# w_out, g and w_in in one buffer, with layer 2's places 64 bytes further on, in a retention and two-layer kernel

## The chip, the cores and the metric

One core of a Trainium2 chip (trn2) runs the whole program. The metric is device time in microseconds (us) from start to end of one execution; lower is better.

## The reference

Retention attention (4 batches, 8 heads, 576 positions, head size 64) gives x, 2304 tokens by 512; two feed-forward layers follow. All is float32 for the caller.

```python
scores = scale * np.matmul(q, k.transpose(0, 1, 3, 2))
x = np.matmul(scores * Dmat, v)        # Dmat: gamma ** (row - column), 0 above the diagonal
h = x @ w_in;  g = np.maximum(0.01 * h, h);  x = g @ w_out       # layer 1, d_ff = 2048
h = x @ w_in2; g = h - np.tanh(h);           out = g @ w_out2    # layer 2
```

The weights come as float64 words and are narrowed to float32 on the chip.

## The kernel before

Every float32 product of the layers is made of three matmuls on float32r parts: a high part times a high part, high times low, low times high. So each tile of w_in, w_out and g holds two parts of 512 columns (1,024 floats, 4 KB a partition). x lies in `xh` and `xl`, 4 planes of 2,304 tokens, for the whole program; `acc` holds the sums of a layer over groups.

The d_ff axis is cut into 16 slices of 128, in 4 groups of 4 (`GF`). A step is one (layer m, group g, token block, slice f). Token blocks are 512 wide, and one is 256 wide (tokens 2048 to 2303). `h_mm` (L255, matmul at L262) makes h of a step with 12 matmuls: weights are w_in, the streamed operand is x. `act_a` (L330) and `chain` (L362) make g on ScalarE, VectorE and GpSimd. `o_mm` (L381, matmul at L404) multiplies with w_out: in layer 1 the weights are w_out and g is streamed (512 or 256 columns); in layer 2 the weights are parts of g and w_out is streamed (512 columns). `evac` (L439) adds the result to acc, after the last slice of a group.

In layer 2 the 512-wide blocks from token 512 on are *folded* (`h_folded`, L268): two steps' h are made together from sums of x's and w_in's parts, with 256-column matmuls at L296, in runs of 6, 12 or 18, and the pending `o_mm` is issued in halves between them (L958 to L987). The folded sums of x are formed from acc by `fold_x` (L411, L427 to L430).

The order on TensorE is the loop at L938: for each step h_mm, then the pending o_mm `lag` steps back (2 in layer 1, 3 in layer 2, `due` at L925), then evac and the planned pieces of weight work. During retention (L517) the first 6 x 256 tokens of group 0 of layer 1 are already done in units (`unit_h`, L721; `unit_o`, L746) between the pairs of heads.

Places in SBUF: `wi` (L80) holds 8 tiles of w_in and 64 spare floats; `w_place` (L82) gives layer 2's tiles, and those of layer 1's group 0, a lead of `LEAD` = 16 floats (64 bytes), the others none. w_out has a ring of 4 tiles (`wring`), g one of 3 (`g1`), and retention's g one of 2 (`g0`), each from its own pool. All these tiles have sizes that are multiples of 128 bytes.

Raw float64 pieces come by DMA on the SP queue (`load_piece`, L127). Those of layer 1's group 0 land in a part of acc that isn't used yet (from token 1280 on); all others in staging pools: `stage` (2 tiles) while retention runs, `stage1` (3 tiles) in the layers. `narrow_ops` (L138) narrows a piece: ScalarE at L152, VectorE at L158, L163 and twice at L169. `split_into` (L241) makes the two parts on ScalarE (L242) and GpSimd (L243). Eight pieces of layer 2's w_out (`early_kept`, L247) are narrowed and split during retention and written to DRAM (`keep_out`, L188), to be fetched again in layer 2 (`fetch`, L218).

Of the kernel before, what the change touches and what calls it, by code (L numbers as in the profile page):

```python
# [35 lines left out]
def retention_moe_moe(  # L36
# [27 lines left out]
    NG = NF // GF  # L64

    keep = ctx.enter_context(tc.tile_pool(name="keep", bufs=1))
    wring = ctx.enter_context(tc.tile_pool(name="wring", bufs=GF))
    ctx.enter_context(tc.tile_pool(name="edge", bufs=1, side="right")).tile(
        [P, 80], F32, name="edge"
    )  # L70
    pools = {}
    narrow = ctx.enter_context(ExitStack())
    pools["st"] = narrow.enter_context(tc.tile_pool(name="stage", bufs=2, side="right"))

    qb = keep.tile([P, 4], F32, name="qb")
    xh = keep.tile([P, KK, NT], F32R, name="xh")
    xl = keep.tile([P, KK, NT], F32R, name="xl")
    acc = keep.tile([P, KK * NT], F32, name="acc")
    acc_t = acc.rearrange("p (d t) -> p d t", d=KK)
    wi = keep.tile([P, 8 * 1024 + 64], F32R, name="wi")  # L80

    def w_place(m, g, j):  # L82
        at = (4 + j) * 1024 if m == 0 else j * 1024
        at += LEAD if m or g == 0 else 0
        return wi[:, at:at + 1024].rearrange("p (i c) -> p i c", i=2)

    HALF = 256
    xe, early_tiles = {}, {}
# [27 lines left out]
    def lag(s):  # L116
        return 2 if steps[s][0] == 0 else 3
# [9 lines left out]
    def load_piece(key):  # L127
        m, kind, f = key
        src = ((w1i, w1o), (w2i, w2o))[m][kind][f]
        if m or key[2] >= GF:  # L130
            st = pools["st"].tile([P, 512], I64 if wide else F32, tag="st", name="st")
        else:
            spare = acc_t[:, len(raw_at) % 4, NT - (1024 if wide else 512):]
            raw_at[key] = st = spare.bitcast(I64 if wide else F32)
        nc.sync.dma_start(out=st, in_=src)
        raw[key] = st

    def narrow_ops(key):  # L138

        if not wide:  # L140
            def only():
                w = cw_pool[0].tile([P, 512], F32, tag="cw", name="cw")
                nc.vector.tensor_copy(out=w, in_=raw.pop(key))
                half[key] = w
            return [only]
        t = {}

        def begin():
            words = raw.pop(key).bitcast(U32).rearrange("p (n t) -> p n t", t=2)
            t["lo"], t["hi"] = words[:, :, 0], words[:, :, 1]  # L150
            t["w"] = cw_pool[0].tile([P, 512], U32, tag="cw", name="cw")
            nc.scalar.activation(  # L152
                out=t["w"].bitcast(F32), in_=t["hi"].bitcast(F32), func=AF.Abs
            )

        def clamp():
            wf = t["w"].bitcast(F32)
            nc.vector.tensor_scalar(  # L158
                out=wf, in0=wf, scalar1=F64_LO, scalar2=F64_HI, op0=ALU.max, op1=ALU.min
            )  # L160

        def shift():
            nc.vector.tensor_scalar(  # L163
                out=t["w"], in0=t["w"], scalar1=3, scalar2=0x3FFFFFF8,
                op0=ALU.logical_shift_left, op1=ALU.bitwise_and,
            )

        def join(src, scalar, op):
            nc.vector.scalar_tensor_tensor(  # L169
                out=t["w"], in0=t[src], scalar=scalar, in1=t["w"], op0=op, op1=ALU.bitwise_or  # L170
            )

        def top():
            join("hi", 0xC0000000, ALU.bitwise_and)

        def low():
            join("lo", 29, ALU.logical_shift_right)
            half[key] = t["w"].bitcast(F32)

        return [begin, clamp, shift, top, low]  # L180

    def keep_split(key, wf):
        at = len(kept) % 4 * 1024
        sp = wi[:, at:at + 1024].rearrange("p (i c) -> p i c", i=2)
        split_into(sp, wf)
        kept[key] = sp

# [30 lines left out]
    def fetch(key):  # L218
        if len(key) == 2:
            j, f = key  # L220
            wp = w_place(1, 0, f % GF // 2 * 4 + 2 + j)
            ws.setdefault(f, {})[j] = wp
        else:
            m, kind, f = key
            wp = wt[key] = (
                wring.tile([P, 2, 512], F32R, tag="wo", name="wp") if kind
                else w_place(1, 0, f % GF // 2 * 4 + f % 2)
            )
        nc.sync.dma_start(out=wp.bitcast(F32), in_=kept[key])

    def split_piece(key):
        wf = half.pop(key)
        m, kind, f = key
        if kind:
            wp = wring.tile([P, 2, 512], F32R, tag="wo", name="wp")
        else:
            wp = w_place(m, f // GF, f % GF)
        split_into(wp, wf)
        wt[key] = wp
# [28 lines left out]
    def h_folded(s):  # L268
# [58 lines left out]

        return first, first_rest, first_sum, second, second_sum, third, fourth

    def act_a(s, tight=False):  # L330
        m, g, t0, n, f = steps[s]
        W, tp = pools["w"], pools["t"]
        h = hp[s][:, :n]
        if m == 0:
            gt = pools["g"].tile([P, 2, W], F32R, tag="g", name="g")
            nc.scalar.activation(out=gt[:, 0, :n], in_=h, func=AF.Prelu, alpha=0.01)  # L336
            nc.scalar.activation(out=h, in_=h, func=AF.Prelu, alpha=0.01)
            tmp[s] = gt
            return
        u = tp.tile([P, W], F32, tag="u", name="u", bufs=3)  # L340
        v = u if tight else tp.tile([P, W], F32, tag="u", name="v", bufs=3)
        q = pools["t2"].tile([P, W], F32, tag="q", name="q", bufs=1)
        t_, mk = early_tiles.pop(s, None) or [
            pools["t2"].tile([P, W], F32, tag=x, name=x) for x in ("t", "mk")
        ]
        nc.scalar.activation(out=u[:, :n], in_=h, func=AF.Square)  # L346
        nc.scalar.activation(out=t_[:, :n], in_=h, func=AF.Tanh)  # L347

        def cube():
            nc.gpsimd.tensor_tensor(out=v[:, :n], in0=t_[:, :n], in1=u[:, :n], op=ALU.mult)  # L350

        if not tight:
            cube()
        nc.scalar.activation(
            out=q[:, :n], in_=u[:, :n], func=AF.Square, scale=math.sqrt(RHO_C), bias=qb[:, 0:1]
        )
        nc.scalar.activation(out=mk[:, :n], in_=u[:, :n], func=AF.Relu, bias=qb[:, 1:2])
        if tight:
            cube()
        tmp[s] = (v, t_, q, mk)  # L360

    def chain(s):  # L362
        m, g, t0, n, f = steps[s]
        h = hp.pop(s)[:, :n]
        if m == 0:
            v, gt = h, tmp.pop(s)
        else:
            v, t_, q, mk = (x[:, :n] for x in tmp.pop(s))
            nc.vector.tensor_tensor(out=h, in0=h, in1=t_, op=ALU.subtract)  # L369
            nc.vector.scalar_tensor_tensor(  # L370
                out=v, in0=q, scalar=RHO_A, in1=v, op0=ALU.add, op1=ALU.mult
            )
            nc.vector.copy_predicated(out=v, mask=mk.bitcast(U32), data=h)  # L373
            gt = pools["g"].tile([P, 2, pools["w"]], F32R, tag="g", name="g")
            nc.scalar.activation(out=gt[:, 0, :n], in_=v, func=AF.Copy)  # L375
        (nc.gpsimd if m else nc.vector).tensor_tensor(  # L376
            out=gt[:, 1, :n], in0=v, in1=gt[:, 0, :n].bitcast(F32), op=ALU.subtract
        )
        ga[s] = gt

    def o_mm(s, part=None):  # L381
# [12 lines left out]
        for d in {None: range(cnt), 0: range(cnt // 2), 1: range(cnt // 2, cnt)}[part]:  # L394
# [2 lines left out]
            o = ps[d // pack][:, at:at + width]  # L397
            for i, (wi, gi) in enumerate(((0, 0), (0, 1), (1, 0))):
                if m == 0:
                    l, r = w[:, wi, ds], gt[:, gi, :n]  # L400
                else:
                    l, r = gt[:, gi, ds], w[:, wi, :]

                nc.tensor.matmul(  # L404
                    out=o, lhsT=l, rhs=r,
                    start=f == 0 and i == 0 and d % pack == 0,
                    stop=f == GF - 1 and i == 2 and (d + 1) % pack == 0,
                    skip_group_check=pack > 1,
                )
# [107 lines left out]
    def retention():  # L517
        with ExitStack() as ac:
            ak = ac.enter_context(tc.tile_pool(name="ak", bufs=1))
            ap_ = ac.enter_context(tc.tile_pool(name="ap", bufs=3))  # L520
            g0_ = ac.enter_context(tc.tile_pool(name="g0", bufs=2))
            cw_pool[0] = ac.enter_context(tc.tile_pool(name="c0", bufs=2))
            ps_s = ac.enter_context(tc.tile_pool(name="ps_s", bufs=1, space=PSUM))
            ps_a = ac.enter_context(tc.tile_pool(name="ps_a0", bufs=1, space=PSUM))
# [189 lines left out]
            def unit_h(u):  # L714
                t0, f0 = place(u)
                for f in range(2):
                    w = wt[0, 0, f0 + f]
                    for kk in range(KK):
                        cs = slice(kk * P, (kk + 1) * P)
                        for j, (wi, x) in enumerate(((0, xh), (0, xl), (1, xh))):  # L720
# [2 lines left out]
                                start=f == 0 and kk == 0 and j == 0,  # L723
                                stop=f == 1 and kk == KK - 1 and j == 2, skip_group_check=True,
                            )
                gt = g0_.tile([P, 2, 2, QW], F32R, tag="g", name="g")
                nc.scalar.activation(out=gt[:, 0], in_=x_b, func=AF.Prelu, alpha=0.01)
                nc.scalar.activation(out=x_b, in_=x_b, func=AF.Prelu, alpha=0.01)
                nc.vector.tensor_tensor(
# [117 lines left out]
    def layers():  # L847
        with ExitStack() as mc:
            pools["t"] = mc.enter_context(tc.tile_pool(name="t1", bufs=2))
            pools["g"] = mc.enter_context(tc.tile_pool(name="g1", bufs=3))  # L850
            pools["st"] = narrow.enter_context(tc.tile_pool(name="stage1", bufs=3, side="right"))
            cw_pool[0] = narrow.enter_context(
                tc.tile_pool(name="c1", bufs=2 * GF + 4, side="right")
# [69 lines left out]
            done = [n_early]  # L923

            def due(s):  # L925
                return n_early <= done[0] <= s - lag(s) and done[0] < end - GF

            def extras(s, quick):
                ops = plan.get(s, [])
# [134 lines left out]
```

## Time and profile before

| | |
|---|---|
| time, median of 3 runs | 876.88 us (876.71 to 878.21) |
| time of the profiled execution | 876.76 us |
| its span, first to last instruction | 875.0 us |
| TensorE (PE) busy | 857.5 us, 98% |
| VectorE, ScalarE, GpSimd busy | 587.6, 445.6, 365.0 us |
| DMA, mean over the span | 125 GB/s |

The profile is one execution. PE is TensorE's matmul, PEld its weight load, which runs beside it; a matmul's recorded duration overlaps the next one's, so PE's pace is read from how far apart matmuls start. The granted clock is 9 tenths or more of 2.4 GHz in all 40 slices of the page, 0.999 in the mean.

### The profile page before, as it was taken

What the parts mean: (1) busy time and instruction counts of PE and PEld (TensorE: products, weight loads), DVE (VectorE), ACT (ScalarE), POOL (GpSimd) and SP (SyncE); (2) the same over time, 40 slices, a digit from 0 to 9 for tenths busy, and PEclk for the clock granted to TensorE, in tenths of its full rate; (3) what the DMA queues carried; (4) which work ended last, traced back from release to release, by engine and by line L of the source; (5) the groups of instructions that cost most, each with busy time, mean ns of one, the idle gap of its engine ahead of it and who ended that gap; (6) DMA issues with size and microseconds to landing.
All of it is one profiled execution on the core that took longest, in us unless ns stands there. A gap on an engine that the chain in (4) does not pass through costs nothing.

```text
span 875.0 us, 14820 instructions
## 1 busy us (share of the span) xinstructions
PE 857.5 (98%) x5584; PEld 744.8 (85%) x5584; DVE 587.6 (67%) x1006; ACT 445.6 (51%) x888; POOL 365.0 (42%) x297
## 2 busy tenths in 40 slices
PE   6999999999999999999999999999999999999997
PEld 5889999888988888888888888888898889889886
DVE  5996776687685777658745567754666566656665
ACT  4553454453345334454534566665666556665663
POOL 2642222140046203273334756554455545453553
PEclk9999999999999999999999999999999999999999
DMA  9835663333455433654534200260004300261112
GB/s 336 316 120 181 207 206 133 133 120 121 145 193 209 153 120 108 230 193 114 208 111 145 97 1 1 73 211 7 1 25 146 119 1 1 73 217 49 49 49 73
DMA packets 36471, 109.23 MB, mean 125 GB/s; under 512 B 4144, under 2 KB 5680, under 8 KB 36400
## 3 DMA queue, kind: packets, MB, share of 16 engines
q1 hardware_dynamic: 35968, 108.08, 35.9%
q8 instruction: 44, 0.72, 0.3%
q10 hardware_dynamic: 432, 0.20, 0.1%
q14 instruction: 27, 0.22, 0.1%
HBM read 78.39 MB, written 29.88 MB: 124 GB/s over the span
## 4 chain that ended last, share of the span: by engine, by line
PE 89%; DVE 5%; DMA 2%; issue 1%; POOL 1%; ACT 1%; SPq 0%; POOLq 0%; DVEq 0%; ACTq 0%
PE a L404 40%; PE h L262 26%; PE h L296 12%; PE a L746 3%; PE x_b L721 3%; PE o L671 1%; DMA cm_sb<-in_cmask 1%; PE sc L595 1%; PE o L660 1%; DVE cw L169 1%; DMA acc<-in_w1i 1%; DVE pt L609 1%; PE x_c L628 0%; DVE acc L467 0%; DVE xl L482 0%
## 5 line engine op out<-in xcount | busy, mean ns | idle before, releaser
L262 PE MATMUL h<-xh,wi 128*128 128x512 f32 (+1 forms) x800 | 229.7, 356 | 0.0
L404 PE MATMUL a<-wp,g 128*128 128x512 f32 x864 | 220.4, 393 | 0.9 <-POOL g L376 0.5
L404 PEld LDWEIGHTS a<-wp,g 128*128 128x128 f32 x864 | 154.5, 188 | 29.5 <-POOL g L376 1.2
L243 POOL TENSOR_TENSOR wi<-cw,wi 128x512 fp32r<-128x512 f32 x64 | 89.8, 1420 | 214.0 <-ACT wi L242 188.3
L404 PE MATMUL a<-g,wp 128*128 128x512 f32 (+1 forms) x816 | 175.9, 364 | 0.6 <-DVE g L376 0.6
L404 PEld LDWEIGHTS a<-g,wp 128*128 128x128 f32 x816 | 141.4, 189 | 25.6 <-DVE g L376 0.8
L262 PEld LDWEIGHTS h<-xh,wi 128*128 128x128 f32 x800 | 143.6, 188 | 22.5
L262 PE MATMUL h<-xl,wi 128*128 128x512 f32 (+1 forms) x400 | 142.4, 356 | 0.0
L350 POOL TENSOR_TENSOR v<-t,u 128x512 f32<-128x512 f32 (+1 forms) x76 | 92.4, 1216 | 92.4 <-ACT t L347 90.5
L376 POOL TENSOR_TENSOR g<-v,g 128x512 fp32r<-128x512 f32 (+1 forms) x76 | 95.7, 1259 | 80.8 <-ACT g L375 80.8
L336 ACT ACTIVATE g<-h 128x512 fp32r<-128x512 f32 (+1 forms) x68 | 37.2, 548 | 166.4 <-PE h L262 124.5
L169 DVE SCALAR_TENSOR_TENSOR cw<-st,cw 128x512 uint32<-128x512 uint32 x112 | 99.0, 884 | 2.9
L370 DVE SCALAR_TENSOR_TENSOR v<-q,v 128x512 f32<-128x512 f32 (+1 forms) x76 | 54.7, 720 | 49.9 <-POOL v L350 49.6
L262 PEld LDWEIGHTS h<-xl,wi 128*128 128x128 f32 x400 | 75.5, 189 | 11.4
L467 DVE TENSOR_TENSOR acc<-a,acc 128x512 f32<-128x512 f32 (+1 forms) x114 | 70.9, 658 | 21.0 <-PE a L404 21.0
L375 ACT ACTIVATE g<-v 128x512 fp32r<-128x512 f32 (+1 forms) x76 | 45.4, 597 | 75.5 <-DVE v L373 68.1
L346 ACT ACTIVATE u<-h 128x512 f32<-128x512 f32 (+1 forms) x80 | 44.0, 550 | 78.0 <-DVE h L290 53.9
L296 PE MATMUL h<-xh,wi 128*128 128x256 f32 x384 | 75.6, 281 | 0.5 <-DVE v L373 0.3
L369 DVE TENSOR_TENSOR h<-h,t 128x512 f32<-128x512 f32 (+1 forms) x80 | 51.5, 644 | 33.7 <-ACT t L347 32.9
L158 DVE TENSOR_SCALAR cw<-cw 128x512 f32<-128x512 f32 x64 | 34.1, 533 | 57.8 <-ACT cw L152 57.7
L296 PEld LDWEIGHTS h<-xe,wi 128*128 128x128 f32 x432 | 60.2, 188 | 8.5 <-DVE mk L290 2.4
L296 PEld LDWEIGHTS h<-xh,wi 128*128 128x128 f32 x384 | 61.9, 188 | 2.9 <-DVE v L373 1.8
(86 smaller groups left out, 1244.5 us busy)
## 6 DMA issues: line engine op xcount, KB each, us to landing
kept<-wi SPq DMA_DIRECT2D x48, 512.0 KB, 3.9
wi<-kept SPq DMA_DIRECT2D x32, 512.0 KB, 4.6
st<-in_w2o SPq DMA_DIRECT2D x16, 512.0 KB, 5.9
st<-in_w2i SPq DMA_DIRECT2D x16, 512.0 KB, 3.7
wp<-kept SPq DMA_DIRECT2D x16, 512.0 KB, 3.7
st<-in_w1i SPq DMA_DIRECT2D x12, 512.0 KB, 4.3
st<-in_w1o SPq DMA_DIRECT2D x12, 512.0 KB, 3.4
kv<-in_vn SPq DMA_DIRECT2D x16, 320.0 KB, 5.3
```

Source lines behind the costliest of these rows:

```text
L169: nc.vector.scalar_tensor_tensor(out=t["w"], in0=t[src], scalar=scalar, in1=t["w"], op0=op, op1=ALU.bitwise_or)
L243: nc.gpsimd.tensor_tensor(out=wp[:, 1, :], in0=wf, in1=wp[:, 0, :].bitcast(F32), op=ALU.subtract)
L262: nc.tensor.matmul(out=ps[:, :n], lhsT=w[:, wi, cs], rhs=x[:, kk, t0:t0 + n], start=kk == 0 and i == 0, stop=kk == KK - 1 and i == 2,)
L296: nc.tensor.matmul(out=out_, lhsT=w[:, wi_, at:at + P], rhs=x(xi, kk), start=start and kk == 0 and j == 0, stop=stop and kk == 1 and j == ...
L346: nc.scalar.activation(out=u[:, :n], in_=h, func=AF.Square)
L350: nc.gpsimd.tensor_tensor(out=v[:, :n], in0=t_[:, :n], in1=u[:, :n], op=ALU.mult)
L369: nc.vector.tensor_tensor(out=h, in0=h, in1=t_, op=ALU.subtract)
L370: nc.vector.scalar_tensor_tensor(out=v, in0=q, scalar=RHO_A, in1=v, op0=ALU.add, op1=ALU.mult)
L375: nc.scalar.activation(out=gt[:, 0, :n], in_=v, func=AF.Copy)
L376: (nc.gpsimd if m else nc.vector).tensor_tensor(out=gt[:, 1, :n], in0=v, in1=gt[:, 0, :n].bitcast(F32), op=ALU.subtract)
L404: nc.tensor.matmul(out=o, lhsT=l, rhs=r, start=f == 0 and i == 0 and d % pack == 0, stop=f == GF - 1 and i == 2 and (d + 1) % pack == 0, s ...
L467: nc.vector.tensor_tensor(out=dst, in0=a, in1=dst, op=ALU.add)
```

## The change

`wi`, `wring`, `g0` and `g1` become one tile `w` of 15 slots of 1,024 floats and a lead: 4 for w_out, 3 for g, 8 for w_in. w_out's and g's slots are taken in turn by two counters. In layer 2 both are used with the lead of 16 floats, as w_in already was; in layer 1 without. A g of a 256-wide block of layer 1 is written with the lead inside its slot; retention's g takes two of the g slots, with the lead. The raw pieces of `early_kept` land in acc's last 512 tokens, each over two planes, in two turns, and the pool `stage` goes. `due` takes the lag from the pending step's layer and not from the current one's.

```diff
--- before.py
+++ after.py
@@ -64,25 +64,36 @@
     NG = NF // GF
 
     keep = ctx.enter_context(tc.tile_pool(name="keep", bufs=1))
-    wring = ctx.enter_context(tc.tile_pool(name="wring", bufs=GF))
     ctx.enter_context(tc.tile_pool(name="edge", bufs=1, side="right")).tile(
         [P, 80], F32, name="edge"
     )
     pools = {}
     narrow = ctx.enter_context(ExitStack())
-    pools["st"] = narrow.enter_context(tc.tile_pool(name="stage", bufs=2, side="right"))
 
     qb = keep.tile([P, 4], F32, name="qb")
     xh = keep.tile([P, KK, NT], F32R, name="xh")
     xl = keep.tile([P, KK, NT], F32R, name="xl")
     acc = keep.tile([P, KK * NT], F32, name="acc")
     acc_t = acc.rearrange("p (d t) -> p d t", d=KK)
-    wi = keep.tile([P, 8 * 1024 + 64], F32R, name="wi")
+    N_OUT, N_G, N_IN = GF, 3, 8
+    wide_all = keep.tile([P, (N_OUT + N_G + N_IN) * 1024 + LEAD], F32R, name="w")
+
+    def slot(k, lead):
+        at = k * 1024 + (LEAD if lead else 0)
+        return wide_all[:, at:at + 1024].rearrange("p (i c) -> p i c", i=2)
 
     def w_place(m, g, j):
-        at = (4 + j) * 1024 if m == 0 else j * 1024
-        at += LEAD if m or g == 0 else 0
-        return wi[:, at:at + 1024].rearrange("p (i c) -> p i c", i=2)
+        return slot(N_OUT + N_G + (4 + j if m == 0 else j), m or g == 0)
+
+    turn = {"o": 0, "g": 0}
+
+    def w_out_place(m):
+        turn["o"] += 1
+        return slot((turn["o"] - 1) % N_OUT, m)
+
+    def g_place(m):
+        turn["g"] += 1
+        return slot(N_OUT + (turn["g"] - 1) % N_G, m)
 
     HALF = 256
     xe, early_tiles = {}, {}
@@ -127,11 +138,20 @@
     def load_piece(key):
         m, kind, f = key
         src = ((w1i, w1o), (w2i, w2o))[m][kind][f]
-        if m or key[2] >= GF:
+        if key in early_kept:
+            k = 2 * (len(raw_at) % 2)
+            raw_at[key] = True
+            if wide:
+                st = acc_t[:, k:k + 2, NT - 512:].bitcast(I64)
+                src = src.rearrange("p (a n) -> p a n", a=2)
+            else:
+                st = acc_t[:, k, NT - 512:]
+        elif m or key[2] >= GF:
             st = pools["st"].tile([P, 512], I64 if wide else F32, tag="st", name="st")
         else:
             spare = acc_t[:, len(raw_at) % 4, NT - (1024 if wide else 512):]
-            raw_at[key] = st = spare.bitcast(I64 if wide else F32)
+            raw_at[key] = True
+            st = spare.bitcast(I64 if wide else F32)
         nc.sync.dma_start(out=st, in_=src)
         raw[key] = st
 
@@ -146,11 +166,17 @@
         t = {}
 
         def begin():
-            words = raw.pop(key).bitcast(U32).rearrange("p (n t) -> p n t", t=2)
-            t["lo"], t["hi"] = words[:, :, 0], words[:, :, 1]
-            t["w"] = cw_pool[0].tile([P, 512], U32, tag="cw", name="cw")
+            st = raw.pop(key).bitcast(U32)
+            t["w"] = t["as"] = cw_pool[0].tile([P, 512], U32, tag="cw", name="cw")
+            if len(st.shape) == 3:
+                words = st.rearrange("p a (n t) -> p a n t", t=2)
+                t["lo"], t["hi"] = words[:, :, :, 0], words[:, :, :, 1]
+                t["as"] = t["w"].rearrange("p (a n) -> p a n", a=2)
+            else:
+                words = st.rearrange("p (n t) -> p n t", t=2)
+                t["lo"], t["hi"] = words[:, :, 0], words[:, :, 1]
             nc.scalar.activation(
-                out=t["w"].bitcast(F32), in_=t["hi"].bitcast(F32), func=AF.Abs
+                out=t["as"].bitcast(F32), in_=t["hi"].bitcast(F32), func=AF.Abs
             )
 
         def clamp():
@@ -167,7 +193,7 @@
 
         def join(src, scalar, op):
             nc.vector.scalar_tensor_tensor(
-                out=t["w"], in0=t[src], scalar=scalar, in1=t["w"], op0=op, op1=ALU.bitwise_or
+                out=t["as"], in0=t[src], scalar=scalar, in1=t["as"], op0=op, op1=ALU.bitwise_or
             )
 
         def top():
@@ -180,8 +206,7 @@
         return [begin, clamp, shift, top, low]
 
     def keep_split(key, wf):
-        at = len(kept) % 4 * 1024
-        sp = wi[:, at:at + 1024].rearrange("p (i c) -> p i c", i=2)
+        sp = slot(N_OUT + N_G + len(kept) % 4, False)
         split_into(sp, wf)
         kept[key] = sp
 
@@ -223,7 +248,7 @@
         else:
             m, kind, f = key
             wp = wt[key] = (
-                wring.tile([P, 2, 512], F32R, tag="wo", name="wp") if kind
+                w_out_place(m) if kind
                 else w_place(1, 0, f % GF // 2 * 4 + f % 2)
             )
         nc.sync.dma_start(out=wp.bitcast(F32), in_=kept[key])
@@ -232,7 +257,7 @@
         wf = half.pop(key)
         m, kind, f = key
         if kind:
-            wp = wring.tile([P, 2, 512], F32R, tag="wo", name="wp")
+            wp = w_out_place(m)
         else:
             wp = w_place(m, f // GF, f % GF)
         split_into(wp, wf)
@@ -327,13 +352,18 @@
 
         return first, first_rest, first_sum, second, second_sum, third, fourth
 
+    def g_at(s):
+        m, g, t0, n, f = steps[s]
+        at = LEAD if m == 0 and n < 512 else 0
+        return slice(at, at + n)
+
     def act_a(s, tight=False):
         m, g, t0, n, f = steps[s]
         W, tp = pools["w"], pools["t"]
         h = hp[s][:, :n]
         if m == 0:
-            gt = pools["g"].tile([P, 2, W], F32R, tag="g", name="g")
-            nc.scalar.activation(out=gt[:, 0, :n], in_=h, func=AF.Prelu, alpha=0.01)
+            gt = g_place(m)
+            nc.scalar.activation(out=gt[:, 0, g_at(s)], in_=h, func=AF.Prelu, alpha=0.01)
             nc.scalar.activation(out=h, in_=h, func=AF.Prelu, alpha=0.01)
             tmp[s] = gt
             return
@@ -371,10 +401,10 @@
                 out=v, in0=q, scalar=RHO_A, in1=v, op0=ALU.add, op1=ALU.mult
             )
             nc.vector.copy_predicated(out=v, mask=mk.bitcast(U32), data=h)
-            gt = pools["g"].tile([P, 2, pools["w"]], F32R, tag="g", name="g")
-            nc.scalar.activation(out=gt[:, 0, :n], in_=v, func=AF.Copy)
+            gt = g_place(m)
+            nc.scalar.activation(out=gt[:, 0, g_at(s)], in_=v, func=AF.Copy)
         (nc.gpsimd if m else nc.vector).tensor_tensor(
-            out=gt[:, 1, :n], in0=v, in1=gt[:, 0, :n].bitcast(F32), op=ALU.subtract
+            out=gt[:, 1, g_at(s)], in0=v, in1=gt[:, 0, g_at(s)].bitcast(F32), op=ALU.subtract
         )
         ga[s] = gt
 
@@ -397,7 +427,7 @@
             o = ps[d // pack][:, at:at + width]
             for i, (wi, gi) in enumerate(((0, 0), (0, 1), (1, 0))):
                 if m == 0:
-                    l, r = w[:, wi, ds], gt[:, gi, :n]
+                    l, r = w[:, wi, ds], gt[:, gi, g_at(s)]
                 else:
                     l, r = gt[:, gi, ds], w[:, wi, :]
 
@@ -518,7 +548,6 @@
         with ExitStack() as ac:
             ak = ac.enter_context(tc.tile_pool(name="ak", bufs=1))
             ap_ = ac.enter_context(tc.tile_pool(name="ap", bufs=3))
-            g0_ = ac.enter_context(tc.tile_pool(name="g0", bufs=2))
             cw_pool[0] = ac.enter_context(tc.tile_pool(name="c0", bufs=2))
             ps_s = ac.enter_context(tc.tile_pool(name="ps_s", bufs=1, space=PSUM))
             ps_a = ac.enter_context(tc.tile_pool(name="ps_a0", bufs=1, space=PSUM))
@@ -723,7 +752,7 @@
                                 start=f == 0 and kk == 0 and j == 0,
                                 stop=f == 1 and kk == KK - 1 and j == 2, skip_group_check=True,
                             )
-                gt = g0_.tile([P, 2, 2, QW], F32R, tag="g", name="g")
+                gt = slot(N_OUT + u % 2, True).rearrange("p i (f n) -> p i f n", f=2)
                 nc.scalar.activation(out=gt[:, 0], in_=x_b, func=AF.Prelu, alpha=0.01)
                 nc.scalar.activation(out=x_b, in_=x_b, func=AF.Prelu, alpha=0.01)
                 nc.vector.tensor_tensor(
@@ -847,7 +876,6 @@
     def layers():
         with ExitStack() as mc:
             pools["t"] = mc.enter_context(tc.tile_pool(name="t1", bufs=2))
-            pools["g"] = mc.enter_context(tc.tile_pool(name="g1", bufs=3))
             pools["st"] = narrow.enter_context(tc.tile_pool(name="stage1", bufs=3, side="right"))
             cw_pool[0] = narrow.enter_context(
                 tc.tile_pool(name="c1", bufs=2 * GF + 4, side="right")
@@ -923,7 +951,7 @@
             done = [n_early]
 
             def due(s):
-                return n_early <= done[0] <= s - lag(s) and done[0] < end - GF
+                return n_early <= done[0] <= s - lag(done[0]) and done[0] < end - GF
 
             def extras(s, quick):
                 ops = plan.get(s, [])
```

## Rows read from the trace of the kernel before

**Rows 1.** The page's head, and its part 1: busy time, share of the span, instructions.

```profile
span 875.0 us, 14820 instructions
PE 857.5 (98%) x5584; PEld 744.8 (85%) x5584; DVE 587.6 (67%) x1006; ACT 445.6 (51%) x888; POOL 365.0 (42%) x297
```

**Rows 2.** Page, part 4: the chain that ended last, shares of the span.

```profile
PE 89%; DVE 5%; DMA 2%; issue 1%; POOL 1%; ACT 1%; SPq 0%; POOLq 0%; DVEq 0%; ACTq 0%
PE a L404 40%; PE h L262 26%; PE h L296 12%; PE a L746 3%; PE x_b L721 3%; PE o L671 1%; DMA cm_sb<-in_cmask 1%; PE sc L595 1%; PE o L660 1%; DVE cw L169 1%; DMA acc<-in_w1i 1%; DVE pt L609 1%; PE x_c L628 0%; DVE acc L467 0%; DVE xl L482 0%
```

**Rows 3.** Groups by line and shape, TensorE: count, busy us, mean ns, idle before.

```profile
L404 PE MATMUL a<-wp,g 128*128 128x512 f32 x864 | 220.4, 393 | 0.9 <-POOL g L376 0.5 <-ACT acc L463 0.4
...
L296 PE MATMUL h<-xh,wi 128*128 128x256 f32 x384 | 75.6, 281 | 0.5 <-DVE v L373 0.3
L296 PE MATMUL h<-xe,wi 128*128 128x256 f32 x432 | 63.1, 282 | 1.0 <-DVE mk L290 1.0
L296 PE MATMUL h<-xl,wi 128*128 128x256 f32 x192 | 53.8, 280 | 0.0
...
L404 PE MATMUL a<-g,wp 128*128 128x256 f32 x192 | 25.8, 283 | 0.6 <-DVE g L376 0.6
```

**Rows 4.** Chain in order of time (start us, us, what), layer 1's long stretch.

```profile
186.82 2.72 PE a L404 x12
189.54 2.72 PE h L262 x12
```

**Rows 5.** The same chain, layer 1's group 0.

```profile
150.75 4.09 PE h L262 x36
154.85 1.44 PE a L404 x12
156.29 1.42 PE h L262 x12
...
167.58 2.80 PE h L262 x12
170.38 2.73 PE a L404 x12
```

**Rows 6.** The same chain, layer 1, around a 256-wide block.

```profile
412.71 2.75 PE h L262 x12
415.46 1.43 PE a L404 x12
```

**Rows 7.** The same chain, folded blocks of layer 2.

```profile
638.15 1.39 PE a L404 x6
639.54 1.42 PE h L296 x12
...
642.34 0.71 PE h L296 x6
```

**Rows 8.** The same chain, the first folded block of layer 2.

```profile
512.33 1.36 PE h L296 x12
513.70 0.70 PE a L404 x3
514.39 0.68 PE h L296 x6
```

**Rows 9.** The same chain, where layer 1 meets layer 2.

```profile
475.50 5.60 PE h L262 x24
481.10 2.75 PE a L404 x12
```

**Rows 10.** Instructions on acc and st, to 160 us: duration ns min/median/max, first and last start.

```profile
L169 DVE SCALAR_TENSOR_TENSOR cw<-acc,cw x16: 681/758/1670, 16.3 to 62.1; 128x512 uint32<-128x512 uint32 x16
...
L135 SPq DMA_DIRECT2D st<-in_w2o x8: 328/368/430, 70.8 to 132.9; - x8
```

**Rows 11.** Waits of TensorE, 505 to 540 us: us in total, times, longest.

```profile
PE h L296 <- DVE mk L290: 1.0, 1, 1.0
PE h L296 <- DVE v L373: 0.3, 1, 0.3
```

## Prediction

> **What bounds the kernel now.** I read the page's head first: of a span of 875.0 us TensorE is busy for 98% [rows 1]. Then the chain of work that ended last: PE holds 89% of it, and three lines alone 78%: L404 (g times w_out), L262 (x times w_in), L296 (layer 2's folded x times w_in) [rows 2]. So a wait elsewhere is worth little, and what counts is the time from one matmul's start to the next. The durations in the groups don't give it, because matmuls overlap (they stand at 281 to 393 ns [rows 3]); the pieces of the chain do, since each names how many matmuls ran in a row and for how long.
>
> I call a place *plain* if it lies a multiple of 128 bytes from the start of xh, and *led* if it lies 64 bytes further. By the declared sizes xh, xl, xe, the w_out ring and layers' g are plain; w_in is led in layer 2 and in layer 1's first group, else plain. What the chain shows, per matmul:
> - 512 columns, weights and streamed operand both plain, long stretch: 2.72 / 12 = 227 ns [rows 4].
> - 512 columns, x plain with led w_in: 2.80 / 12 = 233 ns [rows 5].
> - 256 columns, both plain: 1.44 / 12 = 120 ns; x plain with led w_in: 1.42 / 12 = 118 ns, and in one long stretch 4.09 / 36 = 113.6 ns [rows 5].
> - Layer 2's L404, both plain, in runs of six between L296's runs: 1.39 / 6 = 231 ns, though the same pair of places took 227 in layer 1 [rows 7].
>
> So the pairing of places has a price that differs in sign between 256 and 512 columns, and a change of regime costs something once: a run of twelve after 256-column work takes 2.75 instead of 2.72, in layer 1 too, where nothing is led [rows 4, 6]. The same pairing also has two speeds: L296's twelve took 1.36 after a run of three L404 and 1.42 after a run of six [rows 7, 8].
>
> **The change part by part.** *Layer 1's 256-column L404.* g moves to a led place against plain w_out. There are 192 such matmuls [rows 3], in 16 runs of twelve. From 120 to 118 ns, as led against plain reads beside them, is 16 x 0.02 = 0.3 us; from 120 to 113.6 would be 192 x 6.4 ns = 1.2 us. The first two runs follow directly on the 113.6 stretch [rows 5], so I take 0.5 us, with 0 and 1.2 as ends. All of it lies on the path, as PE is the chain there.
>
> *Layer 2's L404.* w_out and g both become led. The pair stays alike, so a settled run should still take 227. What differs is the seam to L296 and L262, whose w_in is led already and whose x stays plain. Before, the weights' place jumps at each seam and the streamed operand's doesn't; after, the streamed operand's jumps and the weights' doesn't. No row of before shows this seam. There are 128 runs by the loops at L938 to L993 (32 whole steps, 96 halves), and a six costs 1.39 against 6 x 0.227 = 1.36, a twelve 2.75 against 2.72: 0.03 each, some 3.5 us in all [rows 4, 7, 9]. The cheapest entry into alike 512-column work that follows other work is 2.73, after led w_in with 512 columns [rows 5]: 0.01. I take that value, because the weights' jump at the seam is what goes and this is the one row in which an entry was cheap; leaving out the 18 runs cut to three, about 110 runs x 0.02 = 2.2 us. The ends are 128 x 0.03 = 3.8 us gained and, with every one of the 864 matmuls at the 233 ns of the led row instead of 231, 2.0 us lost.
>
> *L296 in layer 2.* Its own places don't move, but what it enters from does. It has 384 + 432 + 192 = 1008 matmuls [rows 3]. At 113.6 instead of 118 they would give 1008 x 4.4 ns = 4.4 us; at 120 they would cost 2.2 us. I take 0, since the regime of 118 follows nearly every settled run now, and the run before stays settled.
>
> *A rule against it.* The rows put 227 and 233 ns on the same 512-column shape [rows 4, 5]. The Trainium skill, "TensorE: Matmul & The Clock Gate", section "Wait — 56ns, not 53.3ns?", has a warm back-to-back matmul start every N / 2.4 GHz plus about 2.5 ns, 215.7 ns at 512 columns, with no term for where operands lie; by that rule this whole change is worth nothing. The trace disagrees, as the two rows differ by 6 ns at one clock.
>
> *Raw pieces in acc.* Eight loads land in acc's far columns instead of a stage of their own. The last read of the earlier pieces there is at 62.1 us, and the first of these loads is issued at 70.8 [rows 10], so the new wait on SP has long ended and nothing queued behind it (qk and kv of later pairs) moves; two turns stay two turns. Price 0; with the 8.7 us gap gone, SP's queue would hold up qk.
>
> *One buffer for rings.* Waits for a ring's next tile become waits for the same readers of the same slot. Where layers meet, a led slot also covers the first 64 bytes of the next plain slot, so a w_out load or a g write waits for one more step's matmuls. That step is over by then for the g writes, and the w_out loads are needed three steps later. Price 0, at most one step's idle, 2.7 us.
>
> *Lag taken from the pending step.* At layer 2's first step the pending L404 now runs at once: the stretch of 24 L262 in a row [rows 9] is split, and a step without L404 follows two steps later. The work is the same. All waits of PE on other engines around it are small, 1.0 and 0.3 us [rows 11]. I take 0, with 1.3 us either way as ends.
>
> Sum: -0.5 - 2.2 = -2.7 us on the profiled execution's 876.76, so 874.1. The median of the runs is 876.88, 0.12 above, so 874.2.
>
> **The rivals.** *L296 locks into its faster regime.* For: 1.36 per twelve exists in this very line, and depends on how the run before ended [rows 8]. Against: it shows only after runs cut to three or after a stall. 4.4 us beside layer 1's 0.5 gives 872.0; with the seams cheap too, 869.8.
>
> *The seams cost the same.* For: 2.75 also stands in layer 1, where no place jumps [rows 6], so the cost may come from the switch of 256 to 512 columns alone. Then only layer 1's 0.5 is left: 876.4.
>
> *The change doesn't do what it says*: places have no part, and the speeds come from what ran before, as in the skill's rule. Then 876.9. The rows against it are those of the two 512-column stretches [rows 4, 5].
>
> *Slower: the jump of the streamed operand spoils layer 2.* Place: each seam between L404 and L296. If the stream then never settles within six, L296 pays 120 (+2.2 us) and L404 233 (+2.0), less layer 1's 0.5: 880.6; with half of it, 878.7. It decides from the point where six L296 take 0.72 or more instead of 0.71 and six L404 1.40. For: L404 has not settled in six now. Against: L296 lies at led against plain before and after.
>
> **How the numbers follow.** Chances: forecast 0.35, faster L296 0.13, seams unchanged 0.27, places without part 0.07, spoiled 0.18. I count a change of 0.2% (1.75 us) as what a measurement of this kernel can tell from none: under 875.1 is faster, over 878.6 slower. That gives faster 0.48, same 0.34, slower 0.18. The time is the forecast's, 874.2, with 872.8 to 875.1 as its own range. The range over the cases runs from the locked L296 with cheap seams, 869.9, to a mostly spoiled layer 2, 879.4.
>
> **What would show it.** In the chain of the changed kernel: layer 1's 256-column L404 at 1.36 to 1.42 per twelve instead of 1.44; layer 2's sixes of L404 at 1.36 to 1.37 instead of 1.39, twelves at 2.73; L296's sixes still 0.71 (0.68 is the fast rival, 0.72 the slow one); layer 1's long stretch still 2.72; SP with no new wait near 71 us; PE's waits between 505 and 540 us within 1.3 us of now. I am wrong if layer 2's sixes stay at 1.39, or if a new PE wait stands where layers meet.

## The result, and the profile after

The changed kernel takes 884.71 us (median of 6 runs, 883.24 to 885.28) against 877.99 us (median of 6, 876.71 to 878.21): a ratio of 1.0078 [1.0065, 1.0091]. It is 6.7 us slower. The forecast was 874.2 us, and its range ended at 879.4. The profiled execution took 885.28 us, with a span of 883.5 us and a mean granted clock of 0.991.

Lines have moved: a unit's first matmuls L721 are now L750, its second ones L746 are L775, L262 is L287, L404 is L434, L296 is L321, L135 is L155, L169 is L195, L763 (the addition of a unit's result into acc) is L792, L680 is L709.

The page's head and part 1 of after answer to [rows 1]; of part 2 the row of the granted clock stands here, which was at 9 in all 40 slices before.

```profile
span 883.5 us, 14823 instructions
PE 859.4 (97%) x5584; PEld 748.0 (85%) x5584; DVE 586.9 (66%) x1006; ACT 446.1 (50%) x888; POOL 365.3 (41%) x297
PEclk9997999999999999999999999999999999999999
```

PE is busy 1.9 us longer, but the span is 8.5 us longer, so most of the loss is idle time. The fourth slice (66 to 88 us) has a granted clock of 7 tenths. That is in retention, far ahead of every place on which the prediction put a price, and at the time of the loads that it priced at 0. The first matmuls of the units mark the stretch in both traces. Timeline of PE, before (columns: start us, us, instruction; the first row of each of two successive units):

```profile
70.64 0.38 PE L721 MATMUL x_b<-xh,wi 128*128 128x256 f32 x1
...
80.82 0.38 PE L721 MATMUL x_b<-xh,wi 128*128 128x256 f32 x1
```

The same of after, with the row at which PE starts again after a wait (in brackets the wait in us and what ended it) and two rows behind it:

```profile
71.97 0.38 PE L750 MATMUL x_b<-xh,w 128*128 128x256 f32 x1
...
80.69 0.58 PE L750 MATMUL x_b<-xl,w 128*128 128x256 f32 x1 [7.32 <-DVE xl L709]
81.06 0.63 PE L750 MATMUL x_b<-xh,w 128*128 128x256 f32 x2
...
83.63 0.41 PE L750 MATMUL x_b<-xh,w 128*128 128x256 f32 x1
...
91.84 0.38 PE L750 MATMUL x_b<-xh,w 128*128 128x256 f32 x1
```

After is 1.33 us late at the first of these units, as it was at the unit ahead of it; e1 and e2 below, with the same wait, aren't (their units start at 70.32 and 70.39), so this is the execution and not the change. From there to the next it takes 91.84 - 71.97 = 19.87 us where before took 10.18: 9.69 us are lost in this one unit. The waits of 0 to 175 us name it (us in total, times, longest):

```profile
DVE acc L792 <- DMA acc<-in_w2o: 11.2, 1, 11.2
...
PE x_b L750 <- DVE xl L709: 7.3, 1, 7.3
```

In this stretch before has no wait of an addition into acc for a load. (ScalarE's copies of later units into acc, L794, wait for loads too, 7.5 us in three waits. TensorE doesn't lose by them: it is 1.33 + 9.69 = 11.0 us late behind this unit, and still 11.0 where the layers start.) The chain of after, in order of time (start us, us, what), says how the one leads to the other:

```profile
69.53 0.29 PE x_e L689 x4
...
69.97 0.33 SPq L579
...
72.19 5.50 DMA acc<-in_w2o
...
77.79 1.29 DVE acc L792 x2
...
79.90 0.74 DVE xl L709 x2
...
80.69 3.36 PE x_b L750 x14
84.05 3.54 PE a L775 x24
```

SP is held by the loads of the next pair of heads (L579), which wait for matmuls of this pair. Then the first raw piece of w_out goes out at 72.19 and lands at 77.69. VectorE has stood idle for 11.2 us by then, since 66.5. The matmuls whose result it is to add (L775) ended at 67.7, so for 10 of the 11.2 us the load alone held the addition. On VectorE `xl` stands behind the addition and starts at 79.90, and the unit on TensorE needs `xl`: it goes on at 80.69. The row of SP's waits shows the mirror image: the second load can't start before the addition is done.

```profile
SPq L155 <- DVE acc L792: 6.2, 1, 6.2
```

The rest of the 9.69 us is the clock. Windows of after (us, then PE, PEld, DVE, ACT, POOL busy with counts, granted clock, DMA share, GB/s):

```profile
74.00:81.00 7.00, 0.32 (x1) 0.32 (x2) 3.08 (x9) 0.67 (x1) 0.00 (x0) 0.59 0.47 144
81.00:85.00 4.00, 4.00 (x20) 4.00 (x20) 1.61 (x3) 0.92 (x2) 0.00 (x0) 0.50 0.32 122
```

And of before:

```profile
81.00:85.00 4.00, 4.00 (x36) 4.00 (x37) 3.84 (x10) 2.59 (x6) 1.57 (x2) 1.00 0.58 217
```

After an idle time of 7.3 us the granted clock is 0.50, the lower of its two levels, and 20 matmuls run where 36 did. The 12 matmuls from 81.06 to 83.63 start 214 ns apart, not the 126 ns of before (3.03 us for 24). So the 14 matmuls in 3.36 us cost 14 x (240 - 126) ns = 1.6 us more, the 24 behind them 3.54 against 2.83, 0.7 more: 7.3 + 1.6 + 0.7 = 9.6 of the 9.69 us. (The Trainium skill, "TensorE: Matmul & The Clock Gate", section "Wait — 56ns, not 53.3ns?", has matmuls of N columns start N / 1.2 GHz apart while the array is cold; an estimate from that is 213 ns at 256 columns, and the 214 ns here agree.)

The layers themselves became faster. Their first run of 36 matmuls starts at 161.78 instead of 150.75, 11.0 us late, and the end comes 8.5 us late: 2.5 us are won back. The chain of after, rows that answer to [rows 5 to 9]: group 0 of layer 1 first, then where the layers meet, the first folded block, and folded blocks near the end:

```profile
161.78 4.09 PE h L287 x36
165.87 1.36 PE a L434 x12
167.23 1.42 PE h L287 x12
168.65 1.41 PE a L434 x12
...
181.29 2.75 PE a L434 x12
...
497.40 5.60 PE h L287 x24
503.00 2.76 PE a L434 x12
...
520.94 1.41 PE h L321 x12
522.35 0.68 PE a L434 x3
...
644.82 1.36 PE a L434 x6
...
649.66 1.41 PE h L321 x12
...
652.43 0.71 PE h L321 x6
```

Layer 2's sixes of L434 take 1.36 instead of 1.39, and layer 1's first 256-column runs 1.36 and 1.41 instead of 1.44. The stretch of 24 L287 has moved by 497.40 - 475.50 - 11.0 = 10.9 us, two steps.

### The profile page after: what moved, and what is told of

Same layout as the page of the kernel before. It is cut to its first block, busy times and chain, and to the rows that moved or that the text cites. A ratio compares the mean times of both kernels' runs of the same rounds, so it can differ in the third digit from the quotient of the medians.

```text
span 883.5 us, 14823 instructions
## 1 busy us (share of the span) xinstructions
PE 859.4 (97%) x5584; PEld 748.0 (85%) x5584; DVE 586.9 (66%) x1006; ACT 446.1 (50%) x888; POOL 365.3 (41%) x297
## 4 chain that ended last, share of the span: by engine, by line
PE 88%; DVE 4%; DMA 3%; issue 2%; POOL 1%; ACT 1%; SPq 0%; ACTq 0%; POOLq 0%; DVEq 0%
PE a L434 39%; PE h L287 26%; PE h L321 13%; PE a L775 3%; PE x_b L750 3%; PE o L700 1%; PE sc L624 1%; PE o L689 1%; DMA qk<-in_kT 1%; DVE cw L195 1%; DMA qk<-in_qT 1%; DMA acc<-in_w2o 1%; DMA qt_sb<-in_qtab 1%; DVE acc L497 0%; DVE xl L512 0%
## 5 line engine op out<-in xcount | busy, mean ns | idle before, releaser
L434 PE MATMUL a<-w 128*128 128x512 f32 (+1 forms) x1680 | 393.3, 377 | 1.7 <-DVE w L406 0.6
L434 PEld LDWEIGHTS a<-w 128*128 128x128 f32 x1680 | 295.2, 188 | 53.5 <-POOL w L406 1.3
L287 PE MATMUL h<-xh,w 128*128 128x512 f32 (+1 forms) x800 | 229.8, 356 | 0.0
L268 POOL TENSOR_TENSOR w<-cw,w 128x512 fp32r<-128x512 f32 x80 | 112.7, 1426 | 237.4 <-ACT w L267 218.5
L287 PEld LDWEIGHTS h<-xh,w 128*128 128x128 f32 x800 | 143.6, 188 | 22.8
L287 PE MATMUL h<-xl,w 128*128 128x512 f32 (+1 forms) x400 | 142.2, 356 | 0.0
L406 POOL TENSOR_TENSOR w<-v,w 128x512 fp32r<-128x512 f32 (+1 forms) x76 | 95.6, 1258 | 78.1 <-ACT w L405 78.1
L195 DVE SCALAR_TENSOR_TENSOR cw<-st,cw 128x512 uint32<-128x512 uint32 x96 | 84.5, 880 | 2.5
L287 PEld LDWEIGHTS h<-xl,w 128*128 128x128 f32 x400 | 75.2, 188 | 11.5
L321 PE MATMUL h<-xh,w 128*128 128x256 f32 x384 | 75.7, 281 | 0.3 <-DVE v L403 0.3
L321 PEld LDWEIGHTS h<-xe,w 128*128 128x128 f32 x432 | 60.5, 189 | 8.3 <-DVE mk L315 2.4
L321 PEld LDWEIGHTS h<-xh,w 128*128 128x128 f32 x384 | 62.3, 190 | 2.6 <-DVE v L403 1.6
L321 PE MATMUL h<-xe,w 128*128 128x256 f32 x432 | 63.2, 282 | 1.0 <-DVE mk L315 1.0
```

What stands on the lines that cost most here:

```text
L195: nc.vector.scalar_tensor_tensor(out=t["as"], in0=t[src], scalar=scalar, in1=t["as"], op0=op, op1=ALU.bitwise_or)
L268: nc.gpsimd.tensor_tensor(out=wp[:, 1, :], in0=wf, in1=wp[:, 0, :].bitcast(F32), op=ALU.subtract)
L287: nc.tensor.matmul(out=ps[:, :n], lhsT=w[:, wi, cs], rhs=x[:, kk, t0:t0 + n], start=kk == 0 and i == 0, stop=kk == KK - 1 and i == 2,)
L321: nc.tensor.matmul(out=out_, lhsT=w[:, wi_, at:at + P], rhs=x(xi, kk), start=start and kk == 0 and j == 0, stop=stop and kk == 1 and j == ...
L406: (nc.gpsimd if m else nc.vector).tensor_tensor(out=gt[:, 1, g_at(s)], in0=v, in1=gt[:, 0, g_at(s)].bitcast(F32), op=ALU.subtract)
L434: nc.tensor.matmul(out=o, lhsT=l, rhs=r, start=f == 0 and i == 0 and d % pack == 0, stop=f == GF - 1 and i == 2 and (d + 1) % pack == 0, s ...
```

## The experiments

Each ratio is to the kernel before, run beside it on the same chip: its median was 877.55 us for the first four and 877.34 us for the last four. The first four asked whether the loads in acc are the whole loss, and what of their form makes the wait. Where the load and the addition touch acc, no byte is shared: the loads fill tokens 1792 to 2303 of planes 0 and 1 or 2 and 3, the units' additions tokens 0 to 511, their copies tokens 0 to 1535. (In e1 and e3 a load fills tokens 1280 to 2303 of one plane; that meets the last unit's copy, but still no addition.) My first theory was that a region over two planes is taken for its whole extent.

**e1_one_plane**: the changed kernel, with each raw piece in one plane.

```diff
-            if wide:
-                st = acc_t[:, k:k + 2, NT - 512:].bitcast(I64)
-                src = src.rearrange("p (a n) -> p a n", a=2)
-            else:
-                st = acc_t[:, k, NT - 512:]
+            st = acc_t[:, k, NT - 1024:].bitcast(I64)
```

> The changed kernel, with the raw pieces of the kept weights in one plane of acc (its last 1,024 words, two turns in planes 0 and 2) instead of 512 words in each of two planes; all else of the change stays. Theory A (the two-plane loads and the two-plane additions into acc are made to wait for each other, and that is the whole loss in retention): the wait of VectorE's addition on the load goes (11.2 us before), TensorE's 7.3 us with it, retention ends as in the kernel before, and layer 2 keeps runs of six at 1.36 us, so 874 to 876 us, faster than the kernel before by 2 to 3. Rival B (the loss comes from the moved places of retention's tiles or from its g in shared slots): 883 to 885, with TensorE idle near 74 us as now.

Measured: 883.75 us, 1.0068 [1.0056, 1.0081]. That is rival B's number, and theory A as I put it falls; whether it is also rival B's cause, e2 answers. Waits of 0 to 175 us (L788 is the addition here):

```profile
DVE acc L788 <- DMA acc<-in_w2o: 11.6, 1, 11.6
```

The wait is there with one plane as with two, and PE's idle time behind it too (7.7 us).

**e2_acc_only**: the kernel before, with nothing of the change but the raw pieces in acc.

```diff
-        if m or key[2] >= GF:
+        if key in early_kept:
+            k = 2 * (len(raw_at) % 2)
+            raw_at[key] = True
+            st = acc_t[:, k:k + 2, NT - 512:].bitcast(I64)
+            src = src.rearrange("p (a n) -> p a n", a=2)
+        elif m or key[2] >= GF:
...
```

Not shown: the narrowing reads the piece from two planes, as in the changed kernel.

> The kernel before with one edit of the change alone: raw pieces of the kept weights land in two planes of acc; the rings, g and the lag stay as before. Theory A: the whole retention loss is here without any moved place: 885 to 889 us, VectorE's addition into acc waits 10 us or more for the load once, and TensorE idles 6 to 8 us. Rival B: 877 to 879 us, no such wait.

Measured: 886.92 us, 1.0102 [1.0089, 1.0115], and the same two waits (L774 is the addition here, L732 a unit's first matmuls, L691 forms `xl`):

```profile
DVE acc L774 <- DMA acc<-in_w2o: 11.5, 1, 11.5
...
PE x_b L732 <- DVE xl L691: 7.5, 1, 7.5
```

The whole loss, and more, stands without one place moved: 9.4 us over the kernel before. So rival B is out. What the rest of the change gives back is 886.92 - 884.71 = 2.2 us, or 9.4 - 6.7 = 2.7 with each against the kernel before beside it.

**e3_one_plane_no_lead**: e1, with w_out's and g's places in layer 2 not moved by 64 bytes.

```diff
-        return slot((turn["o"] - 1) % N_OUT, m)
+        return slot((turn["o"] - 1) % N_OUT, 0)
...
-        return slot(N_OUT + (turn["g"] - 1) % N_G, m)
+        return slot(N_OUT + (turn["g"] - 1) % N_G, 0)
```

> The kernel of e1_one_plane with layer 2's w_out and g in plain slots, as before the change. If layer 2's gain is the places at the seam alone: sixes of L404 go back to 1.39 us and twelves to 2.75, so 2.0 to 2.8 us slower than e1_one_plane, some 877 us, with layer 1's 256-column runs still at 1.42. If instead the gain comes with the lag or with the one buffer: sixes stay at 1.36 and the time is e1_one_plane's within 0.5 us.

Measured: 885.87 us, 1.0095 [1.0081, 1.0110], 2.1 us above e1. One six of the chain in layer 2 (L430 is before's L404):

```profile
646.69 1.39 PE a L430 x6
```

With no lead the sixes are back at 1.39.

**e4_lag_only**: the kernel before, with `s - lag(done[0])`.

> The kernel before with the lag taken from the pending step alone. Theory: the work is only reordered at layer 2's first steps, so the time stays within 0.7 us of the kernel before, and TensorE's waits between 505 and 545 us keep their sum within 1 us. Rival: the earlier addition of layer 1's last block feeds the folded sums sooner, and the time falls by 1 us or more; or the empty step costs its 2.7 us.

Measured: 877.01 us, 0.9999 [0.9988, 1.0009]; PE's waits where the layers meet are 1.0 and 0.3 us, as in [rows 11]. The order of the steps there has no price that can be told.

Since one plane did not help, the second theory was about what e1 had left alone: the load's region is declared in elements of 64 bits (`I64`), the additions' in 32 bits. The same bytes can be loaded as `U32`.

**e5_u32_load**: the changed kernel, with the load declared in 32 bits.

```diff
-                st = acc_t[:, k:k + 2, NT - 512:].bitcast(I64)
-                src = src.rearrange("p (a n) -> p a n", a=2)
+                st = acc_t[:, k:k + 2, NT - 512:].bitcast(U32)
+                src = src.bitcast(U32).rearrange("p (a n) -> p a n", a=2)
```

> The changed kernel with one edit: the eight loads into acc are declared as 32-bit words on both sides instead of 64-bit, over the same bytes in the same two planes. Theory A2 (the places in acc never overlap, tokens 0 to 1535 against 1792 to 2303, but with elements of another width the wait is put in all the same): the program then holds no wait of the additions on these loads, TensorE's 7.3 us idle time goes, retention ends within 1 us of the kernel before, layer 2's sixes stay at 1.36 us, and the time is 874 to 876 us, 2 to 3 below the kernel before. Rival B (moved places of retention's tiles, g in shared slots): 881 us or more, with TensorE still idle before 85 us.

Measured: 875.56 us, 0.9976 [0.9967, 0.9984]: 0.2% faster than the kernel before. Tile acc, to 175 us (duration ns min/median/max, first and last start us):

```profile
L155 SPq DMA_DIRECT2D acc<-in_w2o x8: 550/552/685, 71.3 to 133.3; - x8
...
L792 DVE TENSOR_TENSOR acc<-a,acc x4: 678/686/692, 66.8 to 81.3; 128x512 f32<-128x512 f32 x4
```

The additions run from 66.8 us on, before the first load is issued, where after had them at 77.8 to 88.2. The window that had 20 matmuls:

```profile
81.00:85.00 4.00, 4.00 (x39) 3.88 (x36) 3.84 (x10) 2.48 (x7) 1.57 (x2) 1.00 0.67 243
```

**e6_u32_no_lead**: e5, with layer 2's places not moved (the edit of e3).

> The kernel of e5_u32_load with layer 2's w_out and g in plain slots. If the seam's places alone make layer 2's gain: sixes of L404 at 1.39, twelves at 2.75, 2.0 to 2.8 us slower than e5_u32_load, so 876.5 to 878. If not: within 0.5 us of e5_u32_load.

Measured: 877.78 us, 1.0001 [0.9992, 1.0010], 2.2 us above e5. Chain of e6 in layer 2, at its first runs and further on:

```profile
493.51 2.75 PE a L434 x12
496.26 1.42 PE h L287 x12
497.68 2.75 PE a L434 x12
...
637.31 2.12 PE h L321 x18
639.43 1.39 PE a L434 x6
```

The chain of e5 at the same places:

```profile
492.38 2.76 PE a L434 x12
495.14 1.41 PE h L287 x12
496.56 2.72 PE a L434 x12
...
635.58 2.12 PE h L321 x18
637.70 1.36 PE a L434 x6
```

The first twelve of each follows 512-column work (24 L287 in a row) and takes 2.75 and 2.76; the second follows 256-column work and falls from 2.75 to 2.72. L321's 18 are alike in both, and each six of L434 behind them differs by 0.03 us. That is the seam by itself, and the rest of the change (one buffer, acc, lag, layer 1's lead) comes to nothing that can be told (1.0001).

**e7_u32_g256_plain**: e5, with the g of layer 1's 256-wide blocks not moved (`at = 0` in `g_at`).

> The kernel of e5_u32_load with layer 1's 256-column g in a plain place again. Theory: its 16 runs of twelve go from 1.42 back to 1.44 us, so 0.2 to 0.5 us slower than e5_u32_load, less than the measurement can tell; the runs of 512 columns that follow stay as they are. Rival: the seams between 256 and 512 columns in layer 1 change too, and it is 1 us or more.

Measured: 875.56 us, 0.9978 [0.9969, 0.9987], the same as e5. Chain of e7 in layer 1's group 0:

```profile
158.67 1.44 PE a L434 x12
...
171.35 2.73 PE a L434 x12
```

The first two runs of twelve are slower without the lead, both 1.44, against 1.36 and 1.42 in e5, and the next two 1.42 against 1.41; but the 512-column run that follows takes 2.73, and 2.75 in e5. Of the 0.3 us that 16 runs x 0.02 would give nothing is seen in the time, and a difference this small can't be.

**e8_before_u32_acc**: e2, with the load declared in 32 bits.

> The kernel before with the raw pieces of the kept weights in two planes of acc, loaded as 32-bit words. Theory A2: the kernel before's time within 1 us (877 to 878.5), no wait of VectorE's additions on these loads; e2_acc_only, the same but for the declared width, took 886.9. If the loads into acc cost something beyond that wait (a shared resource, a slower load over two planes): 880 or more.

Measured: 877.17 us, 0.9999 [0.9990, 1.0008], where e2 took 886.92. The two differ in nothing but the declared width of eight loads, at both ends of each. Tile acc of e8, to 175 us:

```profile
L140 SPq DMA_DIRECT2D acc<-in_w2o x8: 550/551/676, 70.9 to 132.7; - x8
...
L774 DVE TENSOR_TENSOR acc<-a,acc x4: 678/685/691, 66.5 to 81.8; 128x512 f32<-128x512 f32 x4
```

So landing in acc costs nothing that can be told, and declaring the landing in 64-bit elements costs 9.5 us (9.4 of e2 and -0.2 of e8, each against the kernel before of its batch).

## Why the prediction was wrong

**Raw pieces in acc: this step failed.** It priced the loads at 0 because the earlier raw pieces there had been read by 62.1 us [rows 10]. That is true, and it answers the wrong question: it asked who last read raw pieces, and not who else touches acc at that time. The view of tile acc of before has the row:

```profile
L763 DVE TENSOR_TENSOR acc<-a,acc x4: 679/682/692, 66.4 to 81.2; 128x512 f32<-128x512 f32 x4
...
DMA to landing us min/median/max: 5.7/6.5/7.2
```

Four additions from 66.4 to 81.2 stand on both sides of the first load at 70.8. I took it for granted that regions which share no byte share no wait. A bound from both sides would have been: nothing, if the two are told apart; if they are not, the addition at 66.4 is held until 70.8 + 5.7 = 76.5 at least, 10 us of VectorE, with `xl` and TensorE's next unit behind it. The runs showed 11.2 us on VectorE, 7.3 us of idle PE, 2.3 us of slow clock, 9.5 us in the time. The prediction did name SP as the queue where a wait might come, and held that such a wait "has long ended"; SP did get a new one near 71 us, the 6.2 us of its second load. But the wait that cost time came on VectorE, from a load that stood behind other loads on SP.

None of the four rivals was this one; the one that ended slower put its loss into layer 2's seams, where there was a gain.

**Layer 2's L404: right in kind, and in size partly by luck.** -2.2 us was forecast from 110 runs x 0.02. e6 less e5 is 877.78 - 875.56 = 2.2 us, and e3 less e1 2.1. But the step left a price of 0.01 to each entry, from one row behind 512-column work [rows 5], though [rows 9] has 2.75 behind such work. In the runs the entry behind 256-column work is the one whose price goes, and it goes altogether (a six of 1.36 is 6 x 0.227); behind 512-column work most of it stays (2.74 and 2.76, against 2.75). Worked out from the starts of the matmuls in the traces of e6 and e5, 79 sixes won 2.0 us, the 12 twelves behind 256-column work 0.3, 15 runs of three 0.2 and the 13 twelves behind 512-column work 0.1, while L321 lost 0.3. So it was more per run in fewer runs, less a loss that stood at 0, and the sum came out the same. Whether w_out or g alone would do was not tried. The rule that time is columns by clock plus a constant (the Trainium skill, "TensorE: Matmul & The Clock Gate", section "Wait — 56ns, not 53.3ns?") would have e5 and e6 alike; the runs disagree, by 0.03 us in each six.

**Layer 1's 256-column L404: right in sign, mis-sized.** -0.5 us was forecast. The twelves did fall, from 1.44 to 1.36 and then 1.41, but the entry into 512 columns behind them went from 2.73 to 2.75, and e7 against e5 shows 0.0 us. From the matmuls' starts in these two traces the twelves won 0.3 us, and the entries behind them lost 0.1.

**L296 at 0: right, within 0.3 us.** It stays at 1.41 per twelve and 0.71 per six. What it lost, the 0.3 us above, is small: the quick runs after a run of three, 1.36 and 0.68 in [rows 8], are 1.41 and 0.71 now. The rival in which it locks into that pace everywhere is out.

**One buffer for the rings, and the lag, both at 0: right.** e6 holds all of the change but layer 2's lead and the 64-bit loads, and stands at 1.0001; e4 has the lag alone, at 0.9999. The 24 L262 in a row are found two steps later, as that step put it.

Together: -2.2 (e5 against e6), 0 for the rest (e6), and 9.4 for the loads (e2) make 7.2 us; 6.7 was measured. Without the wait, e5 is 1.8 us under the kernel before, against the 2.7 forecast.

What is shown is that the declared width alone decides about the wait (e2 against e8, after against e5), and that the shape in planes does not (e1). That the build's comparison of two regions goes wrong, or is made safe, when their element widths differ is the reading that fits; how it compares them was not looked into.

## What to carry to other kernels

Before a tile is given a second use, list every instruction that touches it in the stretch, writers and adders too, and price the case in which the build can't tell the regions apart; then look in the first trace for a wait between the two. Declare all accesses to a shared tile in one element width. And when a change has two parts, one meant to win 2 us in many small pieces and one meant to be free, run the free one by itself first.

## What the runs showed of the hardware

Where operands lie in SBUF has a part in the pace of a float32r matmul at one clock: with w_out and g of layer 2 moved by 64 bytes, as w_in there is, sixes of 512 columns take 1.36 us, and without it 1.39 (e5, e6), while the 256-column work between them hardly changes (1.41 or 1.42 per twelve in both). The price sits at the entry into 512-column work. Behind 256-column work it is about 0.03 us a run unmoved (2.75 for a twelve) and nothing that can be seen moved (2.72, as in the long stretch of [rows 4]); behind 512-column work with led w_in most of it stays (2.75 unmoved, 2.74 and 2.76 moved).

One wait of 7.3 us cost TensorE 2.3 us more after it had ended, as the granted clock stood at 0.50 for the next 4 us.
